# A fused attention and softplus MLP kernel: fp32 state products, fewer turns, weights loaded ahead, a new order of steps

## The chip, the cores and the metric

The kernel runs on one core of a Trainium2 chip. Its time is the device time of one execution in microseconds (us), and several executions are timed. The engines are PE (TensorE, matrix products; PEld is its weight load), DVE (VectorE), ACT (ScalarE), POOL (GpSimd) and SP (SyncE, which here only issues DMAs). Each engine works through its own instructions in program order and waits on semaphores for the others.

## The reference: what is computed

Eight batches of eight heads attend between 512 tokens and 32 state rows, both ways; the result, 8 x 544 rows of 512, goes through an MLP with softplus. The two weight matrices arrive as 64-bit floats, tokens and state as 32-bit ones; the result has 32 bits.

```python
scores = scale * x @ state^T            # per batch and head, 512 x 32
xread  = softmax(scores, over state rows) @ state
scores2 = scale * state @ x^T           # 32 x 512
sread  = softmax(scores2, over tokens) @ x
rows   = concatenate([xread, sread])    # 544 rows a batch, 512 columns over the heads
h   = rows @ w_in                       # 512 -> 2048
g   = maximum(h, 0) + log1p(exp(-abs(h)))
out = g @ w_out                         # 2048 -> 512
```

## The kernel before

**Token rows.** For the 512 token rows of a batch the kernel does not form `xread`. It first makes V = state . w_in for each head ("state products"), and then h = V^T a^T, where a is the softmax over the state rows. So the MLP's first product (`gemm1`, L454) has V as its stationary and the transposed attention `aT` as its moving operand. The hidden features are cut into 16 slots of 128 for each batch. A slot is: six products into a PSUM bank `h`, the softplus (three activations on ACT, L438 to L440, and one addition on DVE, L441, which I call the slot's softplus addition), the split of its result into `ghi` and `glo`, and twelve products with `w_out` into four `acc` banks (`gemm2`, L461). Up to three slots wait between the two products.

**Split operands.** PE multiplies a tile of type float32r faster than one of float32, but with fewer bits. So an operand is split into two parts of 12 bits (`split`: a copy to float32r on ACT or POOL, L92 or L85, and the remainder on DVE or POOL, L93), and a product takes three passes, high by high, high by low and low by high (`PASSES`). `MOVED` is a table of names: a step whose name is in it goes to the other engine than the one that the code names first.

**64-bit weights.** `as_f32` turns a block of 64-bit words into float32. One engine scales the high word (L112 on POOL or L114 on ACT), and three DVE operations (L124 to L126) take the sign bit, shift the low word in, and put the fields together; or, for the blocks that `MOVED` names, two DVE operations (L118, L121), a Sign activation (L120) and a product on POOL (L122).

**State products.** w_in is taken in four chunks of 512 hidden features, each of four blocks q of 128 rows. For chunk 0 and batches 0 to 3, `make_v0` multiplies fp32 operands (`QZ`, the padded state, L167 and L176); batches 0 and 1 are copied to SBUF (`vf`), 2 and 3 go to DRAM (`Vd0`). For chunks 1 to 3, and for all chunks of batches 4 to 7, `make_v` splits each head's weights into parts that stand one above the other (`head`, L218 and L219, tiles `zhl` or `R`), multiplies twice by the split state (`product`, L204), copies the bank to `ve` and writes it to DRAM (L210). `fetch_v` brings a batch's chunk back to `vf` in four pieces, and `split_v` splits it (`vhl`). The converted weights are also written to DRAM (`wsc`), for later batches and for the state's own rows.

**Turns.** `w_in` and `w_out` come in during the first two batches, so those take turns by quarters of the hidden features: eight turns of four slots. After each turn the four `acc` banks are copied to, or added to, sums in SBUF (L549, L552).

**Order.** The order of the work is written out by hand, a letter a step: `START` for batches 0 to 2 and the first 32 slots, `BLOCK` for each later batch, `LAST` for the end; `ATT` gives the order of the steps within a batch's attention. A scheduler then sets each engine's own order from it. All DMAs go through SP's queue, in order, each waiting there until its data or its buffer is ready.

## Time and profile before

| | |
|---|---|
| median of 3 runs | 726.08 us (726.03 to 726.4) |
| span of the profiled execution, first to last instruction | 723.7 us |
| PE, PEld busy | 669.6 us (93%), 538.4 us (74%) |
| DVE, ACT, POOL busy | 526.1 us (73%), 484.9 us (67%), 217.2 us (30%) |
| moved by DMA | 89.76 MB, 124 GB/s over the span |
| mean granted TensorE clock | 0.991 |

The page gives no other time of the profiled execution than its span; the runs' time is that of whole executions. "Busy" is the time in which at least one instruction of the engine runs. Products on PE overlap, so one shows some 390 ns where the next starts 227 ns later, and a busy PE need not be at its peak. In rows of groups, the columns are line, engine, operation, out<-in by the program's names, shape and count, then busy time in us and the mean of one in ns, then idle time of the engine ahead of them and who ended it. Names are without the buffer's number: `wout5` and `wout12` read `wout`, `k2` and `k4` read `k`.

### The profile page before, as it was taken

The numbers are of one execution on the slowest core, as the hardware profiler recorded it, in microseconds if no ns is written. First come the engines' busy times: TensorE is split into PE (matmuls) and PEld (weight loads), VectorE is DVE, ScalarE is ACT, GpSimd is POOL, SyncE is SP. The second block draws the span as 40 slices with busy tenths as digits, with TensorE's granted clock in tenths as the row PEclk, the third lists the DMA queues.
The fourth block names the chain that finished last, engine by engine and source line by source line (L and its number), as shares of the span: only waits on it lengthen the run. The fifth ranks groups of instructions, "written<-read, shape, count | busy, mean of one in ns | idle before, by whom it ended". The sixth has DMA issues, their size and how long they took to land.

```text
span 723.7 us, 9466 instructions
## 1 busy us (share of the span) xinstructions
PE 669.6 (93%) x3012; PEld 538.4 (74%) x3012; DVE 526.1 (73%) x881; ACT 484.9 (67%) x897; POOL 217.2 (30%) x218
## 2 busy tenths in 40 slices
PE   3777869799799999999999999999999999999997
PEld 1445657577687787887888888888888889988886
DVE  4889888999999999569874975498558744534322
ACT  3565868576767787778786776667666676656653
POOL 2456466645754421022110411141113101012100
PEclk9999999999999999999999999999999999999999
DMA  8777727565632645436442421141112112522001
GB/s 293 232 230 246 242 92 257 171 211 163 191 95 95 209 140 178 124 102 203 153 131 88 145 59 59 30 146 30 29 30 87 30 30 73 161 87 60 1 0 59
DMA packets 46194, 89.76 MB, mean 124 GB/s; under 512 B 6976, under 2 KB 13888, under 8 KB 46144
## 3 DMA queue, kind: packets, MB, share of 16 engines
q1 hardware_dynamic: 46144, 89.15, 38.7%
q8 instruction: 24, 0.39, 0.2%
q14 instruction: 26, 0.21, 0.1%
HBM read 60.29 MB, written 28.84 MB: 123 GB/s over the span
## 4 chain that ended last, share of the span: by engine, by line
PE 56%; DVE 26%; ACT 5%; issue 5%; DMA 2%; POOL 2%; SPq 0%; DVEq 0%; ACTq 0%; POOLq 0%
PE acc L461 33%; PE h L454 15%; PE h L501 3%; DVE t L441 3%; DVE glo L93 2%; DVE k L93 2%; PE aux L204 2%; DVE zhl L219 2%; DVE wt L126 2%; DVE k L125 2%; DVE vhl L93 2%; DVE k L124 1%; DVE k L328 1%; PE aux L387 1%; ACT t L438 1%
## 5 line engine op out<-in xcount | busy, mean ns | idle before, releaser
L461 PE MATMUL acc<-wout,ghi 128*128 128x512 f32 x1088 | 339.7, 393 | 3.5 <-DVE o L144 1.0
L461 PEld LDWEIGHTS acc<-wout,ghi 128*128 128x128 f32 x1088 | 203.0, 189 | 48.1 <-DVE o L144 2.0
L461 PE MATMUL acc<-wout,glo 128*128 128x512 f32 x544 | 212.4, 391 | 0.8 <-DVE glo L93 0.8
L454 PE MATMUL h<-aT,vhl 128*128 128x512 f32 x768 | 198.4, 397 | 12.2 <-DVE t L441 9.7
L454 PEld LDWEIGHTS h<-aT,vhl 128*128 128x128 f32 x768 | 144.1, 190 | 46.1 <-DVE t L441 9.8
L441 DVE SCALAR_TENSOR_TENSOR t<-h,t 128x512 f32<-128x512 f32 x136 | 93.2, 686 | 91.9 <-ACT t L440 91.2
L438 ACT ACTIVATE t<-h 128x512 f32<-128x512 f32 x136 | 80.8, 595 | 90.6 <-PE h L454 80.0
L461 PEld LDWEIGHTS acc<-wout,glo 128*128 128x128 f32 x544 | 102.5, 188 | 23.1 <-DVE glo L93 1.4
L93 DVE TENSOR_TENSOR glo<-t,ghi 128x512 fp32r<-128x512 f32 x98 | 75.0, 765 | 36.1 <-ACT ghi L92 21.0
L85 POOL TENSOR_SCALAR ghi<-t 128x512 fp32r<-128x512 f32 x51 | 34.5, 676 | 221.8 <-DVE t L441 189.9
L440 ACT ACTIVATE t<-t 128x512 f32<-128x512 f32 x136 | 85.6, 631 | 2.4
L439 ACT ACTIVATE t<-t 128x512 f32<-128x512 f32 x136 | 85.7, 632 | 1.4
L92 ACT CAST ghi<-t 128x512 fp32r<-128x512 f32 x85 | 52.7, 620 | 48.3 <-DVE t L441 37.4
L93 POOL TENSOR_TENSOR glo<-t,ghi 128x512 fp32r<-128x512 f32 x38 | 51.5, 1357 | 103.1 <-ACT ghi L92 93.1
L93 DVE TENSOR_TENSOR vhl<-vf,vhl 128x512 fp32r<-128x512 f32 x70 | 55.3, 792 | 29.7 <-ACT vhl L92 29.2
L92 ACT CAST vhl<-vf 128x512 fp32r<-128x512 f32 x69 | 42.2, 613 | 13.9 <-PE h L501 8.6
L209 ACT COPY ve<-aux 128x512 f32<-128x512 f32 x41 | 23.2, 579 | 3.5 <-PE aux L204 1.9
L204 PE MATMUL aux<-zhl,wout 128*128 128x512 f32 x48 | 16.1, 420 | 10.0 <-DVE ve L207 4.1
L501 PEld LDWEIGHTS h<-sreadT,vhl 128*128 128x128 f32 x192 | 24.1, 191 | 0.6
L501 PE MATMUL h<-sreadT,vhl 128*128 128x256 f32 x192 | 24.3, 283 | 0.0
L219 DVE TENSOR_TENSOR R<-wt,R 64x512 fp32r<-64x512 f32 x32 | 22.5, 704 | 2.4 <-ACT R L218 1.4
L126 DVE SCALAR_TENSOR_TENSOR wt<-k,k 128x512 int32<-128x512 int32 (+1 forms) x30 | 21.9, 730 | 2.2 <-POOL wout L93 1.2
(139 smaller groups left out, 745.9 us busy)
## 6 DMA issues: line engine op xcount, KB each, us to landing
vd<-ve SPq DMA_DIRECT2D x56, 256.0 KB, 2.3
vf<-vd SPq DMA_DIRECT2D x112, 128.0 KB, 2.8
xT<-in_xt_dram SPq DMA_DIRECT2D x16, 512.0 KB, 4.5
x<-in_xn_dram SPq DMA_DIRECT2D x16, 512.0 KB, 3.9
k<-in_w_out_dram SPq DMA_DIRECT2D x16, 512.0 KB, 3.8
k<-in_w_in_dram SPq DMA_DIRECT2D x12, 512.0 KB, 4.3
out_dram<-o SPq DMA_DIRECT2D x24, 256.0 KB, 2.1
wt<-wsc SPq DMA_DIRECT2D x16, 256.0 KB, 3.1
```

Source lines behind the costliest of these rows:

```text
L85: nc.gpsimd.tensor_scalar(dst, src, 1.0, 0.0, ALU.mult, ALU.add)
L92: nc.scalar.copy(hi, src)
L93: vec(*what).tensor_tensor(lo, src, f32(hi), ALU.subtract)
L126: nc.vector.scalar_tensor_tensor(r.bitcast(I32), h2.bitcast(I32), 3, u, ALU.logical_shift_left, ALU.bitwise_or)
L219: vec("R", *what, o).tensor_tensor(r[z], wf[a], f32(r[a]), ALU.subtract)
L438: nc.scalar.activation(t, h, AF.Abs)
L439: nc.scalar.activation(t, t, AF.Exp, scale=-1.0)
L440: nc.scalar.activation(t, t, AF.Ln, bias=1.0)
L441: nc.vector.scalar_tensor_tensor(t, h, 0.0, t, ALU.max, ALU.add)
L454: nc.tensor.matmul(h, Vhl[b, ft // 2][:, vi, g, cs], aT[b][:, ai, g], start=(n == 0), stop=(n == 5))
L461: nc.tensor.matmul(acc[c], g[gi][:, c0:c0 + P], wout[ft][:, wi], start=(ft == first and i == 0), stop=(ft == last and i == 2))
L501: nc.tensor.matmul(h[:, 256 * i:256 * i + 256], Whl[u, i][:, wi, kt, :], sreadT[:, si, kt, :], start=(n == 0), stop=(n == 11))
```

## The change

The change does five things.

1. *fp32 state products* for chunks 1 to 3 of batches 0 to 3 (`make_vf` in place of `make_v(0, ...)`): two fp32 products a block, as in chunk 0, in place of eight of split operands on four heads' halves. The half for batches 0 and 1 is copied to tiles in SBUF, under the names of `wout` buffers that aren't in use yet, and is no longer written to DRAM and fetched; the half for batches 2 and 3 is written in one piece and fetched in two.
2. *Half the turns*: batches 0 and 1 take five turns of 4, 8, 8, 8 and 4 slots in place of eight of 4.
3. *Weights loaded ahead*: new letters `i` and `o` issue the load of the next block of w_in or w_out; conversion takes the oldest one loaded. The first eight half blocks of w_in have eight buffers. Token inputs `x` are loaded by new steps `L` of the attention and no longer at the very start.
4. *Conversion*: one activation (Prelu with a slope of -2^32 for negative values, so that the sign arrives in the exponent's top bit) and two DVE operations, always.
5. *A new order*: `LOADS`, `ATT`, `START`, `BLOCK` (with `BLOCK2` and `BLOCK3` for batches 2 and 3), `LAST` and `MOVED` are all new.

```diff
-START = 'aaagvavavaBavaaavaaaaaaapabvWaWva|vVVVVVbWbV|pbVb|bVbbVbgbgW|VVVgpbb|V|VVbpgVVWbV|bWgbF|gWVWVpbbg|gVp|gVVVV||FgbVpVVV||VVWgVgWVpVVV|WVVg|gVFVWVVggp|V|VVVVVVpggF|gCVp|cg||WgpFcWgpWWcpF||gg|c||cF|cgcccgcpgcpc|g|cccccc|gg|cpcccgc'
+START = 'aavvaaavaaavaavgavaaBoaWaboapbaaobaWvaa|ibvgVbiVoWVbVVVpbiVbbV|bbaVipWo|iVbbggVVV|VoWiiWpbgVV|VbioVb|Vgbpigo|g|Vbb|WpgbgW|oVVi|VVVVVViiVg|bVpg|pWVo|WVVVgVoVVVo|VWgVpV|WiVgo|Vgg|gpop|g|CgV|VoVgcW|ppcg|og|cW|VcVgoWVW|pVcgcpgg|ccc|cgFgccc|gcccc|pcccp|ccgc|cgc'
...
-    def as_f32(t, *what):
+    def as_f32(t, tag="wt"):
...
         h2 = sb("k2", [P, n], bufs=K2)
-        if ("h2",) + what in MOVED:
-            nc.gpsimd.tensor_scalar(h2, f32(hi), 2.0 ** -112, 0.0, ALU.mult, ALU.add)
-        else:
-            nc.scalar.activation(h2, f32(hi), AF.Copy, scale=2.0 ** -112)
...
-        nc.vector.tensor_scalar(u, hi, SIGN, None, ALU.bitwise_and)
-        nc.vector.scalar_tensor_tensor(u, lo, 29, u, ALU.logical_shift_right, ALU.bitwise_or)
-        nc.vector.scalar_tensor_tensor(r.bitcast(I32), h2.bitcast(I32), 3, u,
-                                       ALU.logical_shift_left, ALU.bitwise_or)
+        nc.scalar.activation(h2, f32(hi), AF.Prelu, scale=2.0 ** -112, alpha=-(2.0 ** 32))
+        r = sb(tag, [P, n], bufs=2 if tag == "wt" else 1)
+        u = r.bitcast(I32)
+        nc.vector.tensor_scalar(u, lo, 29, None, ALU.logical_shift_right)
+        nc.vector.scalar_tensor_tensor(u, h2.bitcast(I32), 3, u, ALU.logical_shift_left, ALU.bitwise_or)
         return r
...
-    QZ = [sb("QZ", [P, 4, P]), sb("zhl", [P, 4, P], bufs=2)]
+    VTAGS = {1: ("wout10", "wout11"), 2: ("wout13", "wout14"), 3: ("vf", "vf")}
+    QZ = [sb("QZ", [P, 4, P]), sb("wout15", [P, 4, P])]
...
+    def load_ahead(k):
+        if coming[k]:
+            come[k].append(load_w(coming[k].pop(0)))
+
+    def ahead(k):
+        if not come[k]:
+            load_ahead(k)
+        return come[k].pop(0)
+
+    def make_vf(cs):
+        for c in cs:
+            for b in range(2):
+                Vf[b, c] = sb(VTAGS[c][b], [P, 2, 512], bufs=2 if c == 3 else 1)
+            for q in range(4):
+                wf = as_f32(ahead("in"), tag="wout12" if (4 * c + q) % 3 == 2 else "wt")
+                nc.sync.dma_start(wsc[c][P * q:P * q + P, :], wf)
+                yield
+                pb = aux()
+                nc.tensor.matmul(pb, QZ[0][:, q, :], wf, start=True, stop=True)
+                r = slice(64 * (q % 2), 64 * (q % 2) + 64)
+                for b in range(2):
+                    dst, src = Vf[b, c][r, q // 2], pb[64 * b:64 * b + 64]
+                    if ("vd", c, q, b) in MOVED:
+                        nc.vector.tensor_copy(dst, src)
+                    else:
+                        nc.scalar.copy(dst, src)
+                made["v", c] = q
+                yield
+                pb = aux()
+                nc.tensor.matmul(pb, QZ[1][:, q, :], wf, start=True, stop=True)
+                ve = sb("ve", [P, 512], bufs=2)
+                if ("ve", 0, c, 2 * q + 1) in MOVED:
+                    nc.vector.tensor_copy(ve, pb)
+                else:
+                    nc.scalar.copy(ve, pb)
+                nc.sync.dma_start(Vd[0, c][:, q, :], ve)
+                made[0, c] = q
+                yield
...
-        w = as_f32(load_w(w_out[P * ft:P * ft + P, :]), ft)
+        w = as_f32(ahead("out"))
...
+            if what == "L":
+                load_x(b, g)
...
-    slots = [(b, ft) for f0 in range(0, NFT, QTR) for b in (0, 1) for ft in range(f0, f0 + QTR)]
+    turns = [(0, 0, 1), (1, 0, 2), (0, 1, 3), (1, 2, 4), (0, 3, 4)]
+    slots = [(b, ft) for b, q0, q1 in turns for ft in range(QTR * q0, QTR * q1)]
```

How the new order moves instructions shows best on three queues. First DVE, behind the first slot's softplus addition, where chunk 1 of w_in is converted. Before (`k` are blocks and scratch, `wt` the converted block, `zhl` the split halves):

```order
L124 TENSOR_SCALAR k_120_425<-k_118_421 128x512
L125 SCALAR_TENSOR_TENSOR k_120_425<-k_118_421,k_120_425 128x512
L93 TENSOR_TENSOR glo_391<-t_385,ghi_390 128x512
L126 SCALAR_TENSOR_TENSOR wt_426<-k_119_423,k_120_425 128x512
L118 TENSOR_SCALAR k_126_441<-k_124_437 128x512
L93 TENSOR_TENSOR vhl_631<-vf_130,vhl_631 128x512
L219 TENSOR_TENSOR zhl_432<-wt_426,zhl_432 64x512
L121 SCALAR_TENSOR_TENSOR k_126_441<-k_125_439,k_126_441 128x512
L441 SCALAR_TENSOR_TENSOR t_480<-h_473,t_480 128x512
```

And now, at the same place, between the first and the third slot's addition (L465):

```order
L114 TENSOR_SCALAR wt_396<-k_98_373 128x512
L170 COPY ve_389<-aux_387 128x256
L115 SCALAR_TENSOR_TENSOR wt_396<-k_107_394,wt_396 128x512
L91 TENSOR_TENSOR vhl_445<-vf_120,vhl_445 128x512
L114 TENSOR_SCALAR wout_120_432<-k_110_404 128x512
L465 SCALAR_TENSOR_TENSOR t_476<-h_469,t_476 128x512
L114 TENSOR_SCALAR wt_415<-k_83_314 128x512
L115 SCALAR_TENSOR_TENSOR wout_120_432<-k_119_430,wout_120_432 128x512
L115 SCALAR_TENSOR_TENSOR wt_415<-k_114_413,wt_415 128x512
```

The third operation of a conversion and the remainders of the split halves (L219) are gone; in their place stand further conversions, of the next block of w_in and of w_out.

Second PE, at the products of that chunk. Before, with `zhl` the split weights of one head, `wout` the two parts of the split state (in buffers that `w_out` takes later) and `aux` the bank:

```order
L204 MATMUL aux_497<-zhl_431,wout_114_411 128x512
L204 MATMUL aux_497<-zhl_431,wout_115_412 128x512
L317 MATMUL aux_503<-xT_200,Z_73 128x512 x2
L204 MATMUL aux_526<-zhl_432,wout_114_411 128x512
L204 MATMUL aux_526<-zhl_432,wout_115_412 128x512
L461 MATMUL acc_556<-wout_87_324,glo_391 128x512
L454 MATMUL h_585<-aT_118,vhl_489 128x512 x6
```

Now, with `QZ` and `wout_2` the padded state of batches 0 and 1, and 2 and 3, and `wt` or `wout_120` a converted block:

```order
L478 MATMUL h_514<-aT_113,vhl_445 128x512 x2
L200 MATMUL aux_406<-wt_396,QZ_87 128x512
L211 MATMUL aux_420<-wt_396,wout_2_88 128x512
L478 MATMUL h_514<-aT_113,vhl_445 128x512 x3
L200 MATMUL aux_436<-wout_120_432,QZ_87 128x512
L211 MATMUL aux_440<-wout_120_432,wout_2_88 128x512
L478 MATMUL h_514<-aT_113,vhl_445 128x512
```

Two fp32 products serve a whole block, and they stand between the passes of a slot's first product.

Third SP, from the start. Before:

```order
L274 DMA xT_90<-in_xt_dram 128x1024
L98 DMA k_4_92<-in_w_in_dram 128x256
L98 DMA k_5_94<-in_w_in_dram 128x256
L98 DMA k_6_96<-in_w_in_dram 128x256
L286 DMA Z_73<-in_zp_dram 128x2x64 x2
L279 DMA x_100<-in_xn_dram 128x1024
L616 DMA zhl_89<-in_zq_dram 128x512
L616 DMA QZ_88<-in_zq_dram 128x512
```

Now:

```order
L295 DMA xT_89<-in_xt_dram 128x1024
L307 DMA Z_73<-in_zp_dram 128x2x64 x2
L97 DMA k_4_93<-in_w_in_dram 128x256
L97 DMA k_5_95<-in_w_in_dram 128x256
L295 DMA xT_97<-in_xt_dram 128x1024
L97 DMA k_7_99<-in_w_in_dram 128x256
L97 DMA k_8_101<-in_w_in_dram 128x256
L97 DMA R_103<-in_w_in_dram 128x256
L644 DMA QZ_87<-in_zq_dram 128x512
```

The padded state for the scores (`Z`) and the second half of the transposed tokens (`xT`) now stand ahead of most weights, and the token rows (`x`) behind all of these.

More of the change, by code (lines that the diff above doesn't have):

```diff
@@ L163, in make_v0 @@
             for q in range(4):
-                wt = as_f32(first.pop(0), 0, half, q)
+                k = 4 * half + q
+                wt = as_f32(first.pop(0), tag=f"wout{4 + k}" if k < 6 else "wt")
                 nc.sync.dma_start(wsc[0][P * q:P * q + P, cs], wt)
@@ L181, in make_v0 @@
                     nc.scalar.copy(ve, pb[:, 0:256])
-                nc.sync.dma_start(Vd0[:, q, cs], ve)
+                nc.sync.dma_start(Vd[0, 0][:, q, cs], ve)
                 made["v0", half] = q
                 yield
-    StK = {}
-    def prep_stk(g4, tags):
-        if len(tags) > 1:
-            k = [sb(tag, [P, H, P], F32R) for tag in tags]
-        else:
-            t = sb(tags[0], [P, 2, H, P], F32R)
-            k = [t[:, 0], t[:, 1]]
-        StK[g4] = k
+    coming = {"in": [w_in[c, q] for c in range(1, 4) for q in range(4)],
+              "out": [w_out[P * ft:P * ft + P, :] for ft in range(NFT)]}
@@ new lines, in attention_then_softplus_mlp @@
+    come = {"in": [], "out": []}
+    def load_ahead(k):
[34 more added lines that the diff above has]
+                yield
@@ L430, in split_wout @@
     def split_wout(ft):
-        assert ft < NFT - 2 or all(made[0, c] == H for c in range(1, 4))
+        assert ft < NFT - 1 or all(made[0, c] == 3 for c in range(1, 4))
         wout[ft] = sb(f"wout{ft}", [P, 2, DM], F32R)
-        w = as_f32(load_w(w_out[P * ft:P * ft + P, :]), ft)
+        w = as_f32(ahead("out"))
         split(wout[ft][:, 0], wout[ft][:, 1], w, "wout", ft)
@@ L531, in flush @@
             return
-        first = ft // QTR * QTR if b < 2 else 0
-        last = first + QTR - 1 if b < 2 else NFT - 1
+        first, last = next(r for r in runs.get(b, [(0, NFT - 1)]) if r[0] <= ft <= r[1])
         if ft == first:
@@ L554, in flush @@
                     nc.sync.dma_start(d, p)
-    fetches = [(fetch_w, (ft,)) if b == B else (fetch_v, (b, ft // 4)) for b, ft in slots if b == B or ft % 4 == 0][2:]
+    fetches = [(fetch_w, (ft,)) if b == B else (fetch_v, (b, ft // 4)) for b, ft in slots if b == B or ft % 4 == 0 and b > 1]
     pieces = [(split_w, (ft,)) if b == B else (split_v, (b, ft // 2)) for b, ft in slots if b == B or ft % 2 == 0]
-    wt_tags = [f"wout{NFT - 2 + i}" for i in range(2)]
     first = []
@@ L597, in run @@
                     break
+            elif what in "io":
+                load_ahead({"i": "in", "o": "out"}[what])
             elif what == "g":
@@ L606, in attention_then_softplus_mlp @@
     v0 = make_v0()
-    v_first = chain(lambda: prep_stk(0, wt_tags), lambda: make_v(0, V_ORDER, RTAGS, VLAG[0]))
-    v_second = chain(lambda: prep_stk(1, ["StK"]), lambda: make_v(1, range(4), ["R"], VLAG[1]))
+    v_first = make_vf(range(1, 4))
+    v_second = chain(prep_stk, lambda: make_v(range(4), 2))
     att[0] = attention(0, ATT[0])
```

104 lines of the change are left out of this document (43 added, 61 removed).

## The prediction

> **What bounds the kernel now.** I read the page's 40 slices first, to see whether one engine limits the whole span.
>
> ```profile
> span 723.7 us, 9466 instructions
> ...
> PE   3777869799799999999999999999999999999997
> DVE  4889888999999999569874975498558744534322
> POOL 2456466645754421022110411141113101012100
> ```
>
> It does not: there are two regimes. In the first dozen slices DVE shows 9, PE 6 to 9 and POOL 4 to 7; from about slice 14 on PE shows 9 and DVE falls away. So the next view is busy time by stretch. I cut at the softplus additions (L441, one for each slot of 128 hidden features), because they mark progress on DVE: the first starts at 45.1 us, the thirteenth at 122.7, the thirty-third, batch 2's first, at 234.1.
>
> ```profile
> L441 DVE SCALAR_TENSOR_TENSOR t<-h,t x12: 676/682/692, 45.1 to 115.7; 128x512 f32<-128x512 f32 x12
> L441 DVE SCALAR_TENSOR_TENSOR t<-h,t x32: 668/681/692, 45.1 to 225.3; 128x512 f32<-128x512 f32 x32
> ```
>
> ```profile
> core 0: us, PE busy (x) PEld busy (x) DVE busy (x) ACT busy (x) POOL busy (x), PEclk, DMA share, GB/s
> 0.00:45.10 45.10, 26.30 (x84) 16.69 (x84) 29.76 (x71) 21.21 (x50) 18.98 (x27) 0.92 0.80 258
> 45.10:122.70 77.60, 62.54 (x250) 45.62 (x251) 70.75 (x97) 54.94 (x106) 45.38 (x39) 0.98 0.62 207
> 122.70:234.10 111.40, 99.12 (x426) 77.68 (x426) 106.18 (x163) 74.22 (x138) 62.30 (x54) 0.98 0.49 157
> 234.10:314.30 80.20, 78.22 (x351) 63.04 (x350) 64.36 (x115) 63.45 (x117) 16.78 (x17) 1.00 0.52 166
> 314.30:723.70 409.40, 403.47 (x1906) 335.39 (x1904) 255.07 (x439) 271.07 (x490) 73.75 (x82) 1.00 0.25 76
> ```
>
> The columns of the second fence are stretch, its length, then busy time and instructions of PE, weight load, DVE, ACT and POOL, then the granted clock and the DMA share. In the second and third stretch DVE is busy for 70.8 of 77.6 and 106.2 of 111.4 us; from 314.3 on it is PE, 403.5 of 409.4, and DVE has a third of its time free. The granted clock, 0.92 to 1.00, explains little of it. The chain that ends last, in the window from 45 to 234 us, says the same by line:
>
> ```profile
> by line: issue 10.2%; DVE zhl L219 7.1%; DVE k L125 6.1%; DVE wt L126 6.1%; DVE glo L93 5.8%; DVE t L441 5.8%; PE h L454 5.6%; DVE k L124 4.5%; PE acc L461 3.8%; DVE wout L93 3.3%; DVE k L93 3.2%; DVE vhl L93 3.0%; DMA k<-in_w_in_dram 1.9%;
> ```
>
> L124 to L126 are the conversion of 64-bit weights, L219 the remainders of the weights split for the state products, and both are DVE's. So the place where this change can earn is the first 234 us; in the 490 us after that, work taken from DVE or ACT is hidden under PE, and work added to PE shows in full.
>
> **The change on DVE.** Mean durations of the operations concerned:
>
> ```profile
> L124 DVE TENSOR_SCALAR k<-k 128x512 int32<-128x512 int32 x24 | 14.8, 617 | 0.1
> L125 DVE SCALAR_TENSOR_TENSOR k<-k,k 128x512 int32<-128x512 int32 x24 | 19.8, 826 | 0.3
> L126 DVE SCALAR_TENSOR_TENSOR wt<-k,k 128x512 int32<-128x512 int32 x24 | 19.5, 811 | 2.2 <-POOL wout L93 1.2 <-issue 0.5 <-DVE k L125 0.2
> L126 DVE SCALAR_TENSOR_TENSOR wt<-k,k 128x256 int32<-128x256 int32 x6 | 2.4, 406 | 0.0
> L219 DVE TENSOR_TENSOR zhl<-wt,zhl 64x512 fp32r<-64x512 f32 x16 | 17.3, 1083 | 2.3 <-ACT zhl L218 1.3 <-POOL zhl L85 0.5
> L93 DVE TENSOR_TENSOR wout<-wt,wout 128x512 fp32r<-128x512 f32 x9 | 9.9, 1100 | 1.8 <-ACT wout L92 1.8
> L93 DVE TENSOR_TENSOR glo<-t,ghi 128x512 fp32r<-128x512 f32 x98 | 75.0, 765 | 36.1 <-ACT ghi L92 21.0 <-POOL ghi L85 13.8
> L207 DVE COPY ve<-aux 128x512 f32<-128x512 f32 x15 | 10.1, 678 | 0.2 <-PE aux L204 0.2
> L552 DVE TENSOR_TENSOR StK<-acc,StK 128x512 f32<-128x512 f32 x12 | 7.8, 673 | 0.0
> ```
>
> The conversion of 28 blocks of 512 columns takes three DVE operations in 24 cases and two in 4; the new one always takes two, a shift (as L124) and a shift with or (as L125). That is 24 operations less, at 0.82 us 19.7 us; 6 of 256 columns go as well, at 0.41, 2.5 us. The products of batches 0 to 3 no longer split weights: 16 remainders on DVE at 1.08, 17.3 us. Half the turns leave 12 additions of parked sums instead of 24: 12 at 0.67, 8.1 us. Together 47.6 us, nearly all ahead of 234 us, where DVE has 206.7.
>
> They do not all fall in the same stretch, so I counted the two orders up to the thirteenth softplus addition. Both have 168 DVE rows there (71 and 48 of them ahead of the first), since loading ahead pulls conversions forward. Conversions: shifts 17 to 23 (+6 at 0.62, +3.7), shift-with-or 31 to 23 (-8 at 0.82, -6.6), 256-wide ones -2.4. Split remainders 9 to 0 (-9.7). Remainders of w_out 4 to 9 (+5.5), of the softplus result 7 to 10 (+2.3), evacuations of PSUM 2 to 6 (+2.7), small ones +2. Net -2.5: 100.5 us of busy time becomes 98. Between the thirteenth and the thirty-third the rest falls: 21 shift-with-ors and 11 shifts become 5 and 5 (24.0 to 7.2), 7 remainders at 1.08 and 12 additions go; 106.2 becomes 106.2 - 16.8 - 7.6 - 8.1 = 73.7.
>
> Means hide a second effect, the time that DVE is held up by POOL:
>
> ```profile
> L125 DVE SCALAR_TENSOR_TENSOR k<-k,k x30: 406/685/1668, 7.1 to 190.3; 128x512 int32<-128x512 int32 x24, 128x256 int32<-128x256 int32 x6
> L219 DVE TENSOR_TENSOR zhl<-wt,zhl x16: 685/985/1673, 49.8 to 162.9; 64x512 fp32r<-64x512 f32 x16
> L93 POOL TENSOR_TENSOR glo<-t,ghi x38: 1267/1296/1796, 67.5 to 691.8; 128x512 fp32r<-128x512 f32 x38
> ```
>
> The columns are minimum, median and maximum in ns. An undisturbed shift-with-or takes 685, but some take 1668. The difference, 983, is less than one POOL subtraction, 1267 at least. POOL was busy for 64.4 us of the first 122.7; in the new order only 15 large rows stand there, 9 subtractions or products, 12 us at the median of 1.3, and 6 copies, which take no longer each: 12 to 20 us. So operations that stay get shorter. How much is not in the trace: nothing at the least; at the most the excess of mean over median on what stays in that stretch: 23 shift-with-ors at 0.14, 9 w_out remainders at 0.4 (1100 against the undisturbed 685), some 75 others at 0.07, together 12. I take 7, a little over the middle, as POOL keeps about a quarter of its work.
>
> The Trainium skill, "SBUF — State Buffer", section "Who interferes with whom", says that a DVE instruction with two SBUF inputs and a GpSimd instruction that reads SBUF take one port pair in turn, and that whichever comes second waits until the first is done. By that rule, as an estimate, all 12 us would go with POOL's rows, and the forecast would be 5 us lower. That a held operation exceeds its median by less than one POOL subtraction agrees with it.
>
> **The change on ACT.** The means:
>
> ```profile
> L114 ACT ACTIVATE k<-k 128x512 f32<-128x512 f32 x19 | 12.6, 667 | 2.8 <-DMA k<-in_w_out_dram 2.8
> L218 ACT CAST zhl<-wt 64x512 fp32r<-64x512 f32 x15 | 9.2, 615 | 0.6 <-PE aux L204 0.5
> L209 ACT COPY ve<-aux 128x512 f32<-128x512 f32 x41 | 23.2, 579 | 3.5 <-PE aux L204 1.9 <-DMA vd<-ve 1.0 <-ACT sr L395 0.5
> L327 ACT COPY k<-aux 64x512 f32<-64x512 f32 x24 | 13.9, 578 | 2.2 <-DVE k L328 1.6 <-PE aux L323 0.3
> ```
>
> Ahead of the thirteenth softplus ACT's rows go from 144 to 166: first steps of conversions 11 to 28 (they came partly from POOL), 13 at 0.67 and 4 of half width, +10.4; copies of 64 rows out of the new products, 18 at 0.58 as for the 64-row copy L327, +10.4; split copies -10 at 0.61, -6.2; evacuations -3.4; parked sums -2.4; others +4.5. Net +13: 76.2 becomes 89.5. The activation that carries the sign is priced as the scaling copy that it replaces, 0.67, bounded by ACT's other 512-column work at 0.58 and 0.67. Over the rest of the start ACT loses about 10 of 74.2. The batches after it gain some 8 us of copies from POOL, under PE.
>
> **The change on PE.** It gets dearer.
>
> ```profile
> 11.57 0.59 PE L176 MATMUL acc<-wt,zhl 128*128 128x256 f32 x2
> 12.00 0.59 PE L167 MATMUL acc<-wt,QZ 128*128 128x256 f32 x2
> 560.51 0.61 PE L461 MATMUL acc<-wout,ghi 128*128 128x512 f32 x2
> 561.19 0.61 PE L461 MATMUL acc<-wout,ghi 128*128 128x512 f32 x2
> L204 PE MATMUL aux<-zhl,wout 128*128 128x512 f32 x48 | 16.1, 420 | 10.0 <-DVE ve L207 4.1
> ```
>
> An fp32 product of 256 columns starts 0.43 us after the last one (11.57, 12.00), so 512 columns take 0.86. Three products of split operands take 0.68 (560.51 to 561.19), 0.227 each. Of 48 split products 24 fp32 ones are left: +20.6 - 10.9 = +9.7 us, 20 of the 24 in the first stretch. There PE's own time, from the order's counts, is 180 split products (40.8), 20 new fp32 ones (17.2), 16 of 256 columns for the first chunk and as many in the read (13.8), 8 scores (6.9) and transposes (2): 81 us. In the next stretch it has 20 slots of 18 products (81.7), 4 fp32 products (3.4) and batch 2's attention (about 6): 91.
>
> **DMA and SP.** Twelve writes of products go, and 48 small fetches become 12 larger ones, for two batches no longer pass through DRAM:
>
> ```profile
> vd<-ve SPq DMA_DIRECT2D x56, 256.0 KB, 2.3
> vf<-vd SPq DMA_DIRECT2D x112, 128.0 KB, 2.8
> ```
>
> That takes 5 us of latency off the first use of a chunk, which DVE's backlog covers today. Loads of x move behind the first conversions, and w_in and w_out are issued some blocks ahead of use. In the first stretch the volume stays about the same: six more blocks of 512 KB against the writes and fetches saved. At 258 and 207 GB/s it fits into a somewhat shorter stretch. I cost all this at nothing; if it does not hold, it is the second rival.
>
> **The sum.** First stretch: DVE 98 - 7 = 91 busy, plus the 22.2 that it idles today (15.3 of them before the first softplus, where it waits for loads and the attention's chain): 113. ACT: 89.5 plus its 24 idle ahead of the first softplus, 113 to 114. PE's 81 is covered. I take 114 against 122.7, with 108 (all blocking gone, first softplus 4 us sooner) and 122 (two engines equally full wait for each other) as ends. Second and third together: PE is now the longest with 91, against DVE 74 and ACT 64. In the stretch from 234.1, where DVE and ACT stand at 64 of 80, PE is busy for 78.2 of 80.2; with attention work crowding the end I take 8 us of loss: 99 against 111.4, ends 94 and 107. The rest I leave at 489.6; its products are the same. So 723.7 - 8.7 - 12.4 = 702.6 for the span. The median of the runs, 726.08, is 2.4 above the span of the profiled execution, and what lies around the span stays: 705.0.
>
> **Rivals.** First, more than that: DVE's start shrinks because the first softplus no longer waits behind 31 us of DVE work, POOL's hold is gone, and PE runs at its own time. With both lower ends, 108 and 94, the span is 691.6 and the time 694. For it speaks how long a held operation takes, 1668 against 685; against it that ACT gets fuller exactly there.
>
> Second, the relief is eaten: with DVE, ACT and PE at 91, 90 and 81 of 114, waits pass from one to the other, or loads come late. The waits of the start show the links:
>
> ```profile
> PE h L454 <- DVE t L441: 9.7, 4, 3.9
> PE aux L204 <- DVE ve L207: 4.1, 4, 1.6
> SPq L210 <- ACT ve L209: 65.4, 27, 6.3
> ```
>
> With 122 and 107 the span is 718.6, the time 721; half that is 713. Against it: PE waited only 4.1 us for copies of the 24 products.
>
> Third, slower, by one mechanism: a converted block now holds its buffer until both fp32 products and the write to DRAM have read it, where a split released it. DVE converts in order, so a block whose buffer is taken stops softplus additions behind it; the products wait for a bank, the bank for ACT's three copies. There are 12 such blocks, and the forecast lies 21 us below today, so from 1.8 us a block on the kernel is slower; if each waits for a whole product and three copies, 0.86 + 3 x 0.58 = 2.6 us, it takes 705 + 31 = 736. Against it: the blocks take turns in three buffers, and SP's queue already waits 65 us for such copies, 27 times, behind which nothing stood still for long.
>
> Fourth, no change: if the start is a chain of latencies and not DVE's fill, the kernel saves perhaps the 10 us of the lighter rows ahead of the first softplus, and PE's 9.7 us eat them: 725 to 727. DVE at 94% from 45 to 234 us (176.9 of 188.9) speaks against it.
>
> **How the numbers follow.** A change within 0.2%, 1.5 us, could not be told from none. The forecast, 698 to 713: 0.55. More than that, below 698: 0.16. Eaten, 713 to 724.6: 0.20. Same: 0.03. Slower: 0.06. So faster 0.91. The range leaves out the worst of the second rival with all of the third and the tail of the first: 693 to 719.
>
> **What would show it.** In the new profile the thirteenth softplus should start near 114 us and the thirty-third near 213; DVE busy near 88 to 100 us in the first of these and near 74 in the next, POOL under 25 in the first; shift-with-or means near 0.70; PE at 9 from about slice 7 on; fp32 products 0.86 apart; stretch after 234 no longer than now. If the thirteenth comes after 120 with DVE idle for over 30, the relief went into waits; if PE idles for over 15 in the next stretch, loads or evacuations took the lead. A second table load on ACT would make all of it wrong.

## Result and profile after

The changed kernel takes 707.63 us (median of 4 runs, 706.78 to 713.27) against 726.06 for the one before (725.87 to 726.4). The ratio of the runs is put at 0.9765, with a 95% interval from 0.973 to 0.9799 (the two medians alone give 0.975). The profiled execution took 708.3 us with a span of 706.3. The prediction said 705.0, with 693 to 719 as its range.

The first lines of the page of the changed kernel, as shown of the one before:

```profile
span 706.3 us, 9196 instructions
...
PE   5679999999999999999999999999999999999997
DVE  4499768936798997796858754875487534544322
...
POOL 1221102665233565201201070107010510000220
```

PE shows 9 from the fourth slice on; before, it did so without a break only from the twelfth on. DVE's unbroken block of 8s and 9s (slices 2 to 16) is broken up, and in the first dozen slices POOL has about half the work that it had.

The softplus additions (now L465) as marks of progress, in two windows that end just ahead of the thirteenth and the thirty-third:

```profile
L465 DVE SCALAR_TENSOR_TENSOR t<-h,t x12: 646/684/692, 39.4 to 112.3; 128x512 f32<-128x512 f32 x12
L465 DVE SCALAR_TENSOR_TENSOR t<-h,t x32: 646/687/692, 39.4 to 205.0; 128x512 f32<-128x512 f32 x32
```

The first starts at 39.4 us (before 45.1). The next after these rows, the thirteenth and the thirty-third, start at 117.8 (122.7) and 211.0 (234.1). Busy time in the stretches between these marks, columns as in the prediction:

```profile
0.00:39.40 39.40, 23.60 (x70) 13.94 (x70) 18.65 (x49) 17.63 (x41) 8.65 (x14) 0.96 0.79 270
39.40:117.80 78.40, 75.43 (x274) 50.21 (x275) 65.00 (x121) 70.91 (x138) 12.04 (x12) 0.98 0.78 253
117.80:211.00 93.20, 93.02 (x414) 75.33 (x413) 68.67 (x114) 64.80 (x118) 42.37 (x40) 1.00 0.28 86
211.00:706.30 495.30, 488.64 (x2258) 396.48 (x2256) 313.96 (x538) 347.98 (x620) 109.77 (x106) 1.00 0.28 90
```

Take PE's idle time, length minus first busy column. Before it was 18.8, 15.1, 12.3 and 7.9 us in the four stretches, 54.1 in all; now it is 15.8, 3.0, 0.2 and 6.7, together 25.6. PE's busy time rose from 669.6 to 680.7. So the change took 28.5 us of waiting from PE and made its busy time 11.1 us longer (4.1 ahead of the thirty-third addition, 7.0 behind it), which makes the 17.4 us by which the span fell. The 23.1 us won at the thirty-third addition are not all kept: the rest of the run takes 495.3 us where it took 489.6. The chain of work that ended last, between 39 and 211 us, by line:

```profile
by line: PE acc L485 38.6%; PE h L478 20.8%; PE aux L200 3.3%; ACT wout L207 3.2%; ACT ghi L90 2.3%; PE aux L211 2.1%; ACT k L111 2.0%; issue 1.9%; ACT t L463 1.9%; ACT t L462 1.8%; ACT t L464 1.7%; PE aux L411 1.2%; PE aux L405 1.1%; DVE k
```

Conversion and remainders on DVE led before; gemm2 (L485) and gemm1 (L478) lead now.

### The profile page after: what moved, and what is told of

Its sections match the earlier page's. It is cut to its first block, busy times and chain, and to the rows that moved or that the text cites. A ratio compares the mean times of both kernels' runs of the same rounds, so it can differ in the third digit from the quotient of the medians.

```text
span 706.3 us, 9196 instructions
## 1 busy us (share of the span) xinstructions
PE 680.7 (96%) x3012; PEld 536.0 (76%) x3012; DVE 466.3 (66%) x818; ACT 501.3 (71%) x914; POOL 172.8 (24%) x170
## 4 chain that ended last, share of the span: by engine, by line
PE 81%; ACT 9%; DVE 7%; issue 2%; DMA 1%; POOL 0%; SPq 0%; ACTq 0%; DVEq 0%; POOLq 0%
PE acc L485 47%; PE h L478 22%; PE h L525 3%; PE aux L235 2%; PE aux L411 1%; ACT t L463 1%; ACT t L462 1%; ACT t L464 1%; ACT ghi L90 1%; PE aux L341 1%; PE aux L347 1%; DVE k L91 1%; PE aux L392 1%; DMA xT<-in_xt_dram 1%; PE aux L200 1%
## 5 line engine op out<-in xcount | busy, mean ns | idle before, releaser
L485 PE MATMUL acc<-wout,ghi 128*128 128x512 f32 x1088 | 343.1, 394 | 0.9 <-DVE StK L577 0.5
L485 PEld LDWEIGHTS acc<-wout,ghi 128*128 128x128 f32 x1088 | 203.2, 188 | 48.2 <-issue 2.4
L485 PE MATMUL acc<-wout,glo 128*128 128x512 f32 x544 | 214.1, 394 | 0.0
L478 PE MATMUL h<-aT,vhl 128*128 128x512 f32 x768 | 203.7, 402 | 4.3 <-DVE t L465 3.8
L478 PEld LDWEIGHTS h<-aT,vhl 128*128 128x128 f32 x768 | 142.2, 189 | 44.4 <-DVE t L465 9.6
L465 DVE SCALAR_TENSOR_TENSOR t<-h,t 128x512 f32<-128x512 f32 x136 | 93.1, 686 | 97.4 <-ACT t L464 97.1
L485 PEld LDWEIGHTS acc<-wout,glo 128*128 128x128 f32 x544 | 102.1, 188 | 22.7 <-issue 0.7
L91 DVE TENSOR_TENSOR glo<-t,ghi 128x512 fp32r<-128x512 f32 x100 | 70.3, 703 | 35.4 <-ACT ghi L90 14.8
L90 ACT CAST ghi<-t 128x512 fp32r<-128x512 f32 x104 | 64.5, 620 | 36.4 <-PE acc L485 23.2
L91 DVE TENSOR_TENSOR vhl<-vf,vhl 128x512 fp32r<-128x512 f32 x62 | 47.1, 760 | 36.0 <-ACT vhl L90 34.0
L83 POOL TENSOR_SCALAR ghi<-t 128x512 fp32r<-128x512 f32 x32 | 21.7, 679 | 180.7 <-PE acc L485 139.8
L91 POOL TENSOR_TENSOR glo<-t,ghi 128x512 fp32r<-128x512 f32 x36 | 48.5, 1351 | 49.6 <-ACT ghi L90 43.1
L90 ACT CAST vhl<-vf 128x512 fp32r<-128x512 f32 x59 | 36.4, 616 | 18.1 <-PE h L525 11.7
L368 POOL TENSOR_TENSOR T<-T,sm 128x512 f32<-128x512 f32 x13 | 15.1, 1160 | 120.7 <-DVE sm L367 92.3
L111 ACT ACTIVATE k<-k 128x512 f32<-128x512 f32 (+1 forms) x32 | 20.2, 645 | 10.3 <-DMA k<-in_w_in_dram 7.7
L352 DVE TENSOR_TENSOR k<-aux,k 64x512 f32<-64x512 f32 x24 | 16.4, 682 | 12.5 <-ACT k L351 12.3
L115 DVE SCALAR_TENSOR_TENSOR wt<-k,wt 128x512 int32<-128x512 int32 (+1 forms) x26 | 20.2, 791 | 2.0 <-ACT k L111 1.7
```

The source lines that it names most:

```text
L83: nc.gpsimd.tensor_scalar(dst, src, 1.0, 0.0, ALU.mult, ALU.add)
L90: nc.scalar.copy(hi, src)
L91: vec(*what).tensor_tensor(lo, src, f32(hi), ALU.subtract)
L111: nc.scalar.activation(h2, f32(hi), AF.Prelu, scale=2.0 ** -112, alpha=-(2.0 ** 32))
L115: nc.vector.scalar_tensor_tensor(u, h2.bitcast(I32), 3, u, ALU.logical_shift_left, ALU.bitwise_or)
L465: nc.vector.scalar_tensor_tensor(t, h, 0.0, t, ALU.max, ALU.add)
```

## Experiments

The theory to test was the prediction's: DVE's fill set the start, and DVE relieved, PE's own time sets it. The kernels below undo or add one part each. A scheduler orders the instructions anew after each edit, so I take differences of 3 us or so between two kernels as possibly its doing. All times are medians; differences are against the 707.63 of the changed kernel unless said otherwise.

**The new conversion alone, in the kernel before.**

```diff
...
-            nc.scalar.activation(h2, f32(hi), AF.Copy, scale=2.0 ** -112)
...
-        nc.vector.tensor_scalar(u, hi, SIGN, None, ALU.bitwise_and)
-        nc.vector.scalar_tensor_tensor(u, lo, 29, u, ALU.logical_shift_right, ALU.bitwise_or)
-        nc.vector.scalar_tensor_tensor(r.bitcast(I32), h2.bitcast(I32), 3, u,
-                                       ALU.logical_shift_left, ALU.bitwise_or)
+        nc.scalar.activation(h2, f32(hi), AF.Prelu, scale=2.0 ** -112, alpha=-(2.0 ** 32))
+        u = r.bitcast(I32)
+        nc.vector.tensor_scalar(u, lo, 29, None, ALU.logical_shift_right)
+        nc.vector.scalar_tensor_tensor(u, h2.bitcast(I32), 3, u, ALU.logical_shift_left, ALU.bitwise_or)
```

> The kernel before with one part of the change alone: the new conversion, one activation and always two DVE operations. Theory (DVE's own time sets the start): DVE loses 24 operations of 0.82 us and 6 of 0.41, 22 us, and POOL 15 copies and 6 products; the thirty-third softplus addition comes 12 to 20 us sooner than 234.1 and the kernel takes 708 to 715. Rival (a chain of loads, products and softplus sets the start, DVE is only full beside it): 722 to 726. Second rival (ACT, which now takes the scalings from POOL, becomes the bound): 726 to 732.

Measured: 720.97 us (720.52 to 722.62), ratio 0.9923 [0.9902, 0.9944], a gain of 5 us where 11 to 18 were expected, and close to the rival's 722. DVE's busy time fell by 29 us in all, from 526.1 to 497.1. In its windows between the first, thirteenth and thirty-third additions:

```profile
48.50:121.70 73.20, 62.65 (x250) 46.07 (x250) 54.64 (x84) 56.52 (x109) 34.64 (x31) 0.95 0.63 218
121.70:231.20 109.50, 100.89 (x425) 78.83 (x426) 97.09 (x153) 74.84 (x138) 58.30 (x51) 0.97 0.48 160
```

DVE is busy for 54.6 of 73.2 us and 97.1 of 109.5, where it had 70.8 of 77.6 and 106.2 of 111.4, and yet the second stretch is only 1.9 us shorter. The shift's group in this kernel says where part of the time went:

```profile
L114 DVE TENSOR_SCALAR wt<-k 128x512 int32<-128x512 int32 x28 | 14.5, 519 | 10.7 <-POOL wout L93 7.4 <-DMA wsc<-wt 2.0 <-POOL zhl L207 1.2
```

The shift now writes the converted block's own buffer, so it waits 10.7 us until earlier readers of it are done, POOL's remainders above all. A DVE that was busy for 94% of a stretch was not its only limit: in the old order most of what it saved became waiting (DVE idles for 223.7 us of this span, 197.6 before). How much of that is this claim on the buffer, and how much the old order, isn't separated.

**The old conversion, in the changed kernel.**

```diff
-        nc.scalar.activation(h2, f32(hi), AF.Prelu, scale=2.0 ** -112, alpha=-(2.0 ** 32))
+        nc.scalar.activation(h2, f32(hi), AF.Copy, scale=2.0 ** -112)
...
-        nc.vector.tensor_scalar(u, lo, 29, None, ALU.logical_shift_right)
+        nc.vector.tensor_scalar(u, hi, -2147483648, None, ALU.bitwise_and)
+        nc.vector.scalar_tensor_tensor(u, lo, 29, u, ALU.logical_shift_right, ALU.bitwise_or)
```

> The changed kernel with the old conversion: a scaling copy on ACT and always three DVE operations, 28 of 512 and 8 of 256 columns more on DVE, 23 us, nearly all ahead of 140 us. Theory (PE and ACT set the changed kernel's start, DVE has 13 of 78 us free in the first stretch): 8 to 14 us slower than the changed kernel, 715 to 721. Rival (DVE no longer matters once PE leads at 39 us): 707 to 710. If DVE is still what counts: 728 to 731.

Measured: 718.85 us (718.13 to 720.26), 0.9892 [0.9871, 0.9913], 11.2 us more.

```profile
41.60:127.30 85.70, 76.76 (x276) 50.22 (x275) 77.69 (x144) 70.44 (x136) 12.93 (x12) 0.98 0.72 234
```

DVE has 17.5 us more in all, and 77.7 of the 85.7 us between the first and the thirteenth addition. So the new conversion is worth 11 us in the new order and 5 in the old one, where it also moved scalings from POOL to ACT.

**Every fp32 product done twice.**

```diff
-                nc.tensor.matmul(pb, QZ[0][:, q, :], wf, start=True, stop=True)
+                for _ in range(2):
+                    nc.tensor.matmul(pb, QZ[0][:, q, :], wf, start=True, stop=True)
...
```

> The changed kernel with each of the 24 fp32 products done twice (same result): PE has 20.6 us more, 17 of them in the first stretch; every other engine has the same work. Theory (from the first softplus on PE is the chain): 15 to 20 us slower than the changed kernel, 722 to 728. Rival (ACT and DVE set the first stretch and PE's 81 us have cover there): 707 to 713.

Measured: 731.98 us (731.05 to 732.46), 1.0069 [1.005, 1.0088], 24.4 us more for 20.6 us of products.

```profile
41.00:140.20 99.20, 94.25 (x320) 59.14 (x321) 70.06 (x127) 75.14 (x141) 12.18 (x13) 0.98 0.66 218
```

The stretch to the thirteenth addition grew from 78.4 to 99.2 us, with PE busy for 94.3 of it. PE has no room there to hide work. Four rows of PE show the price, two products each (two records a product):

```profile
50.09 1.95 PE L201 MATMUL aux<-wt,QZ 128*128 128x512 f32 x4
51.88 1.88 PE L213 MATMUL aux<-wt,wout 128*128 128x512 f32 x4
53.64 1.96 PE L201 MATMUL aux<-wout,QZ 128*128 128x512 f32 x4
55.43 1.96 PE L213 MATMUL aux<-wout,wout 128*128 128x512 f32 x4
```

From 50.09 to 55.43 stand six products, 0.89 us each; the prediction had 0.86.

**One fp32 product a block instead of two.**

```diff
-                pb = aux()
-                nc.tensor.matmul(pb, QZ[1][:, q, :], wf, start=True, stop=True)
```

> The changed kernel with one fp32 product a block in place of two (that for batches 2 and 3 is left out, and their state products are copied from the first one's bank): PE has 10.3 us less, ACT, DVE and the DMAs have the same work. Theory (PE is the chain): 8 to 10 us faster than the changed kernel, 698 to 700. Rival (ACT, with 71 of 78 us in the first stretch, is next to PE): 3 to 5 us faster, 703 to 705.

Measured: 702.49 us (701.47 to 704.22), 0.9671 [0.9648, 0.9695], 5.1 us less for 10.3 us of products.

```profile
38.70:114.10 75.40, 68.24 (x261) 47.90 (x262) 63.54 (x120) 69.48 (x136) 13.19 (x12) 0.98 0.81 270
```

PE now idles for 7.2 us of the stretch, and ACT, with 69.5 of 75.4, is the fullest. So PE leads by some 5 us, and ACT stands next.

**The load of split products, with and without that product.** Both kernels add this to each block, the first on top of the kernel with one product:

```diff
...
+    both = sb("wout15", [P, 2, 512])
...
+    def resplit(wf, o):
+        a, z = slice(64 * o, 64 * o + 64), slice(64 - 64 * o, 128 - 64 * o)
+        r = both[:, 1].bitcast(F32R)
+        nc.scalar.copy(r[a], wf[a])
+        nc.vector.tensor_tensor(r[z], wf[a], f32(r[a]), ALU.subtract)
...
+                for o in range(2 if (4 * c + q) % 3 == 0 else 1):
+                    resplit(wf, o)
```

> The changed kernel with the loads of the old state products: the second fp32 product of each of the 12 blocks left out (batches 2 and 3 get copies of the first bank, as in the earlier kernel with one product), PE -10.3 us, and 16 halves of the converted blocks split into a scratch tile, 16 casts on ACT at 0.61 and 16 remainders on DVE at 0.69 to 1.08, ACT +9.8, DVE +11 to +17. Theory (in the new order the fp32 products pay, since what they free on ACT and DVE counts for more than their 10 us on PE): ACT would need 82 of the first stretch's 78.4 us, so the time is 709 to 716, above the changed kernel's 707.6. Rival (PE's own time decides and the other engines have room): 700 to 706, so that the fp32 products alone cost time.

> The changed kernel with the same 16 casts on ACT and 16 remainders on DVE added and both fp32 products kept: what the split work costs by itself in the new order. Theory (ACT at 70.9 and DVE at 65.0 of 78.4 us are close behind PE there): 8 to 13 us more, 715 to 721, nearly all of it ahead of the thirteenth softplus addition. Rival (hidden beside PE): 707 to 710.

Measured: 715.82 us (713.9 to 718.82), 0.9858 [0.9834, 0.9882], for the first, 8.2 more than the changed kernel; 718.71 (717.63 to 719.09), 0.9892 [0.9878, 0.9906], for the second, 11.1 more. Their stretch between the first and the thirteenth addition, of the first and then of the second:

```profile
41.20:121.70 80.50, 69.91 (x259) 48.57 (x260) 71.87 (x129) 74.51 (x145) 12.83 (x12) 0.96 0.72 235
```

```profile
38.20:125.00 86.80, 79.67 (x274) 53.31 (x275) 73.23 (x132) 76.99 (x149) 13.34 (x12) 0.92 0.70 229
```

In the first, PE idles for 10.6 us, with ACT at 74.5 and DVE at 71.9 of 80.5: the stretch is longer than any engine's busy time in it, and I read this as two engines nearly full that wait for each other. The effects nearly add up: 11.1 for the split work less 5.1 for the product makes 6.0, and 8.2 was measured. The fp32 products cost PE 10 us and still pay.

**POOL made busy again in the first stretch.**

```diff
...
+    both = sb("wout15", [P, 2, 512])
...
+    def hold(c, q):
+        r = slice(64 * (q % 2), 64 * (q % 2) + 64)
+        v = Vf[0, c][r, q // 2]
+        nc.gpsimd.tensor_tensor(both[r, 1], v, v, ALU.mult)
```

It is called three times a block; `both` has the padded state of batches 2 and 3 in its first half, and nothing reads what is written to the second.

> The changed kernel with 36 more POOL products of 64 x 512 (both inputs in SBUF, output unused), three behind each block of the chunks 1 to 3, 47 us of POOL time in the first stretch, where POOL has 66 of 78 us free. Theory (POOL's operations hold DVE's): DVE's shift-with-or and subtractions of the first stretch get longer, means 0.82 to 0.95 against 0.69 undisturbed, DVE's busy time there grows by 8 to 15 us, and the kernel takes 3 to 10 us more than the changed one. Rival (no hold; the long DVE operations have another cause): means as in the changed kernel and 706 to 709.

Measured: 723.77 us (721.7 to 730.56, 10 runs), 0.9965 [0.9938, 0.9992], 16.1 more. The conversion's two groups and the remainders of w_out in the changed kernel, then with POOL busy:

```profile
L115 DVE SCALAR_TENSOR_TENSOR wt<-k,wt 128x512 int32<-128x512 int32 x24 | 19.5, 821 | 2.0 <-ACT k L111 1.7
L91 DVE TENSOR_TENSOR wout<-wt,wout 128x512 fp32r<-128x512 f32 x14 | 12.2, 868 | 3.7 <-POOL wout L83 2.4 <-ACT wout L90 1.2
L114 DVE TENSOR_SCALAR wt<-k 128x512 int32<-128x512 int32 x24 | 11.5, 488 | 2.3 <-PE aux L211 2.2
```

```profile
L115 DVE SCALAR_TENSOR_TENSOR wt<-k,wt 128x512 int32<-128x512 int32 x24 | 22.7, 955 | 0.9 <-ACT k L111 0.7
L114 DVE TENSOR_SCALAR wt<-k 128x512 int32<-128x512 int32 x24 | 19.4, 817 | 0.7 <-PE aux L219 0.7
L91 DVE TENSOR_TENSOR wout<-wt,wout 128x512 fp32r<-128x512 f32 x14 | 15.3, 1089 | 4.3 <-POOL wout L83 3.2 <-ACT wout L90 1.0
```

With the same number of DVE instructions, 818, and 42.6 us more of POOL work, DVE's busy time rose by 17.6 us, 0.41 for each. The trace shows it operation by operation: of the 28 plain shifts (L114) of 512 columns, the 15 that started while POOL was at work took 634 to 1510 ns, the 13 others 404 to 428. DVE's stretch to the thirteenth addition:

```profile
38.80:130.20 91.40, 80.73 (x277) 52.62 (x278) 80.04 (x121) 71.25 (x138) 47.83 (x42) 0.94 0.65 218
```

DVE takes 80.0 us for the 121 instructions that took 65.0. The Trainium skill, "SBUF — State Buffer", "Who interferes with whom", has the two engines share one port pair; that DVE's operations grow when only POOL gets work agrees with it. PE's 5.3 us more of busy time at a granted clock of 0.94 against 0.98 are a part of the 16 us that this doesn't explain.

**Without loading ahead**: the letters `i` and `o` are taken from `START`, so that a block's load is issued where it is converted.

> The changed kernel without the steps that load w_in and w_out ahead: each block of 512 KB is asked for where it is converted; all else, the tables of the order too, stays. Theory (in the first stretch the engines are 83 to 96% full, so each late block stalls DVE and ACT in order): with some 4.8 us to landing and 23 blocks up to the thirteenth softplus, 8 to 25 us slower than the changed kernel, 715 to 732, with waits of DVE and ACT for the weights' DMA. Rival (four buffers and the queue hide the loads, as before the change): 706 to 710.

Measured: 712.39 us (712.16 to 714.66), 0.9812 [0.9789, 0.9836], 4.8 more, less than expected. The first and thirteenth addition come at 37.8 and 117.8 us, no later than in the changed kernel. What is lost is lost where batch 2's attention is made, from the 25th slot's addition to the 29th's:

```profile
165.90:195.50 29.60, 26.22 (x116) 21.60 (x115) 24.09 (x36) 15.77 (x28) 15.24 (x14) 0.94 0.34 108
```

The waits in the same window have this row:

```profile
PE aux L392 <- ACT e L380: 3.4, 1, 3.4
```

PE idles for 3.4 us there, waiting once for an exponential (line, releaser, us in total, times, longest). In the changed kernel the same piece takes 24.3 us and PE is busy for all of it. How the missing letters lead there isn't shown.

**Eight turns again.**

```diff
-    turns = [(0, 0, 1), (1, 0, 2), (0, 1, 3), (1, 2, 4), (0, 3, 4)]
+    turns = [(b, q, q + 1) for q in range(4) for b in (0, 1)]
```

> The changed kernel with the eight turns of four slots of before: 12 more additions of parked sums on DVE (8.1 us) and three more handovers of the four banks. Theory (PE is the chain from 39 us on, DVE has 24 of 93 us free in the second stretch): the additions are hidden, 1 to 4 us slower, 708 to 712. Rival (each handover stalls PE for its copies, since all four banks turn at once): 3 times 2.7 us, 714 to 717.

Measured: 711.0 us (709.48 to 711.85), 0.979 [0.9767, 0.9813], 3.4 more: as expected, though no more than a new order alone can do.

**Products ahead of the first scores.** In the changed kernel PE's first products take twice as long as the same ones later (columns: start, duration, engine, line, count):

```profile
4.95 3.75 PE L341 MATMUL aux<-xT,Z 128*128 128x512 f32 x4 [4.95 <-DMA Z<-in_zp_dram]
9.76 3.54 PE L341 MATMUL aux<-xT,Z 128*128 128x512 f32 x4 [1.05 <-DMA xT<-in_xt_dram]
...
26.50 3.68 PE L405 MATMUL acc<-x,a2T 128*128 128x256 f32 x8 [1.60 <-ACT a2T L395]
...
31.34 1.99 PE L405 MATMUL h<-x,a2T 128*128 128x256 f32 x8 [0.73 <-ACT a2T L395]
33.17 1.88 PE L341 MATMUL aux<-xT,Z 128*128 128x512 f32 x4
```

Two kernels give PE work that nobody reads, so that it doesn't idle. The first one:

```diff
...
-                nc.tensor.matmul(pb[:, 0:256], QZ[1][:, q, :], wt, start=True, stop=True)
+                for _ in range(2 if k < 6 else 1):
+                    nc.tensor.matmul(pb[:, 0:256], QZ[1][:, q, :], wt, start=True, stop=True)
...
+                if b == 0 and g == 0:
+                    pb = aux()
+                    for _ in range(5):
+                        nc.tensor.matmul(pb[:, 0:256], Z4[:, 0, :], xTin[b, g][:, 0, 0:256], start=True, stop=True)
...
+    for _ in range(4):
+        nc.tensor.matmul(pb[:, 0:256], busy[:, 0:P], busy[:, 0:256], start=True, stop=True)
...
```

> The changed kernel with products that nobody reads in PE's gaps of the first 25 us: four on a zeroed tile before the first loads land, five between the scores of the two groups, and the second product of the first six half blocks done twice. Theory (the scores at 5 and 10 us took 3.75 and 3.54 for four halves and the first read 3.68, against 1.88 and 1.99 later, because the granted clock is low after idle stretches, and all three stand on the chain to the first softplus): these take 1.9 to 2.1, the first softplus starts 2 to 4 us sooner, the kernel takes 703 to 706. Rival (loads and DVE set the first softplus, or PE's added work delays what it should speed up): 707 to 710.

Measured: 714.79 us (713.71 to 714.98), 0.9835 [0.9815, 0.9855], 7.2 more. The read did take 1.98 us, but the scheduler put a half-block product ahead of the first gemm1, and PE waited there for its conversion:

```profile
26.11 1.98 PE L410 MATMUL acc<-x,a2T 128*128 128x256 f32 x8
...
40.12 1.22 PE L158 MATMUL acc<-wt,QZ 128*128 128x256 f32 x2 [7.59 <-DVE wt L115]
```

The first softplus addition came at 48.5 us. So I chose repeats that leave PE's order at the start as it was (none between the scores, and `2 <= k < 6`):

> The changed kernel with four products on a zeroed tile ahead of the first scores, and the second product of four of the first chunk's half blocks done twice. In this version, as in the changed kernel, PE takes all but the last two half blocks, then the transposes and the read of the first attention, and only then the first slot; the earlier version had half-block products ahead of the transposes. Theory (the first products run at half speed because PE has idled, and the first softplus addition waits for that chain): scores of 1.9 us in place of 3.75 and 3.54, a read of 2.0 in place of 3.68, the first softplus addition 2 to 4 us sooner, at 35 to 37 us, and the time 703 to 706. Rival (the chain ahead of the first slot is set by loads, conversions and the softmax on DVE and ACT, whose orders move as well): the first softplus addition at 38 to 41 us and the time 706 to 711.

Measured: 707.22 us (706.39 to 707.51), 0.9729 [0.9712, 0.9745]. That interval and the changed kernel's overlap, and the medians are 0.4 us apart; it is no better. The first rows of PE and the first read:

```profile
1.45 3.78 PE L638 MATMUL aux<-a2T 128*128 128x256 f32 x8 [1.45 <-DVE a2T L635]
5.04 2.38 PE L342 MATMUL aux<-xT,Z 128*128 128x512 f32 x4
10.06 1.96 PE L342 MATMUL aux<-xT,Z 128*128 128x512 f32 x4 [2.64 <-DMA xT<-in_xt_dram]
...
25.36 1.99 PE L406 MATMUL acc<-x,a2T 128*128 128x256 f32 x8 [1.34 <-ACT a2T L396]
```

DVE just ahead of the first softplus addition (L466 here):

```profile
37.97 1.03 DVE L114 TENSOR_SCALAR wt<-k 128x512 int32<-128x512 int32 x1
38.92 0.28 DVE L114 TENSOR_SCALAR wt<-o 128x256 int32<-128x256 int32 x1
39.24 0.69 DVE L466 SCALAR_TENSOR_TENSOR t<-h,t 128x512 f32<-128x512 f32 x1
```

The second score and the read run at full speed, the first score nearly so, and the first gemm1 starts at 33.57 us instead of 35.25. But the first softplus addition starts at 39.24, as good as no earlier: two shifts of the conversion had come ahead of it on DVE. So the rival's forecast holds: both scores and the read together take 4.6 us less, of which 1.7 are left at the first gemm1 and next to nothing at the first softplus addition.

**Four copies from ACT to DVE**: `("vd", 1, 0, 1)`, `("vd", 1, 2, 1)`, `("vd", 2, 0, 1)` and `("vd", 2, 2, 1)` are added to `MOVED`.

> The changed kernel with four of the 64-row copies out of the fp32 products (chunks 1 and 2, blocks 0 and 2, batch 1) on DVE in place of ACT: ACT -2.3 us, DVE +2.7 in the first stretch, where they are busy for 70.9 and 65.0 of 78.4. Theory (ACT stands next to PE there, as the kernel with one product a block in place of two showed, which gained 5.1 of 10.3 us): the thirteenth softplus addition 1 to 2 us sooner and the time 705 to 707.5. Rival (PE alone sets that stretch, or DVE's queue holds the copies behind conversions): no gain or a loss of up to 3 us, 707.5 to 711.

Measured: 710.98 us (709.71 to 711.39), 0.9782 [0.9764, 0.98], 3.4 more. The thirteenth addition comes at 118.2. The chain in the window from 39 to 118 us, by line:

```profile
by line: issue 9.4%; PE acc L485 9.0%; DVE wt L115 7.5%; ACT wout L207 6.8%; ACT k L111 5.9%; ACT t L463 5.5%; ACT t L462 4.5%; DVE wt L114 3.9%; PE h L478 3.8%; ACT ghi L90 3.7%; ACT t L464 3.5%; PE aux L405 2.5%; ACT StK L574 2.4%; DVE wo
```

DVE's conversion (L115, L114) stands in it with 11.4%, beside gemm2's 9.0%; in the changed kernel L115 has 2.2% of that window's chain and gemm2 17.5%. That is the rival's forecast, by its second reason. No version tried here that computes the whole result is clearly faster than the changed kernel.

## Why the prediction was right, and where it wasn't

*Where the gain would fall.* Ahead of the thirty-third addition, as said: 23.1 us there, and a loss of 5.7 behind it.

*What sets the start.* The prediction took DVE's own time as the limit. It was one of several. Freed alone, DVE's 29 us gave 5 (first experiment). The gain needs the relief and the new order together; how much the order alone would give wasn't tried.

*First stretch, 114 forecast, 117.8 measured.* The engines came out near the sums: ACT 88.5 busy against 89.5, POOL 20.7 against "under 25", DVE 83.6 against 91. The step that failed is "PE's 81 is covered". From 39.4 us on PE is busy for 75.4 of 78.4, and more products lengthen the run by at least their own time (24.4 for 20.6). PE was busy for 99.0 us of the first 117.8, where 81 were counted. About 5 of the difference are first products that run at half speed, and 5 more that PE had by then done 196 split and 22 fp32 products where 180 and 20 were counted; the rest isn't split up. DVE could end at 114; PE, which also idles for 15.8 us ahead of the first addition, could not.

*Blocking by POOL, 7 us taken of at most 12.* This was too small. At the 0.41 measured, the 43.7 us by which POOL's busy time fell ahead of the thirteenth addition (64.4 to 20.7) are worth 18. From the 98 counted, that gives 80; measured were 83.6. The bound was too low: it gave 0.07 us to each operation outside two groups, but the plain shift took 617 ns on average before, with a median of 419. Nor did the gain come where I looked for it: shift-with-or took 821 ns on average, 826 before, though 0.70 was forecast.

```profile
L115 DVE SCALAR_TENSOR_TENSOR wt<-k,wt x26: 424/691/1780, 36.8 to 139.3; 128x512 int32<-128x512 int32 x24, 128x256 int32<-128x256 int32 x2
```

Half of these took 691 ns or less (the columns are minimum, median and maximum). Of the 28 shift-with-ors of 512 columns six took more than 1 us, and each of these started while a POOL instruction ran; without POOL at work none took more than 695. The Trainium skill's rule, weighed in the prediction, gives the better DVE sum here (86 against the 83.6 measured, where 91 was taken). The time didn't follow, as PE led.

*Second stretch, 99 forecast, 93.2 measured.* DVE 68.7 against 74, ACT 64.8 against 64, and PE 93.0 of 93.2, against an own time of 91. The 8 us set aside for attention work that crowds the end weren't needed. The two misses, +3.8 and -5.8, leave the thirty-third addition at 211.0, forecast 213.

*The rest, 489.6 taken.* This is nearly as large a miss as the second stretch: 495.3. "Its products are the same" was right, but not that they take the same time. The kernel before in that part, to set beside the last of the four rows above:

```profile
234.10:723.70 489.60, 481.68 (x2255) 398.43 (x2253) 319.43 (x553) 334.52 (x606) 90.53 (x99) 1.00 0.29 91
```

At the mark PE still has 2258 products to run, where it had 2255, so the 23.1 us were not won by putting products off past it. But it is busy with them for 488.6 us in place of 481.7: 216.4 ns a product in place of 213.6. It idles for less (6.7 against 7.9), and the granted clock is 1.00 in both. The longer time goes with the new order: the two kernels that keep the old one have 489.6 in that part, the twelve with the new one 493.6 to 496.5. What in the order spaces the products out isn't shown.

*The parts.* Undone one at a time, the conversion is worth 11.2 us, fp32 products against the load of split ones 8.2, loads ahead 4.8 and fewer turns 3.4. That is 27.6, more than the 18.4 of the whole, so they overlap. To put 42.6 us of work back on POOL costs 16.1, more than any of these: by this the relief of POOL, which the prediction had as a term of 7 us, is a large part of the gain, and it overlaps with the conversion, which took scalings off POOL. The conversion's activation costs what the copy did, as said: 675 ns against 667, with one table load in the whole kernel:

```profile
L111 ACT ACTIVATE k<-k 128x512 f32<-128x512 f32 x28 | 18.5, 675 | 2.7 <-DMA k<-in_w_out_dram 2.4 <-DMA k<-in_w_in_dram 0.2
L50 ACT ACT_TABLE_LOAD x1 | 1.3, 1283 | 0.7 <-PEq L696 0.7
```

Loading ahead was costed at nothing; undone, it costs 4.8 us.

*The rivals.* "Eaten" fits the first stretch by its number, 3.8 us more than forecast, but not by its mechanism: PE idles for only 3.0 us from 39.4 to 117.8. "More than that" failed in the first stretch on PE, and held in the second: 93.2, where the lower end was 94. The slower case, blocks that hold their buffers, showed only in small: from 39.4 to 117.8 us a shift of the conversion waits twice on DVE for an fp32 product that still reads its buffer, 2.8 us in all, where the mechanism reckoned with 31. PE waits 0.2 us for the copies of the fp32 products (L207), and 0.9 for a conversion.

```profile
DVE wt L114 <- PE aux L211: 2.2, 1, 2.2
DVE wout L114 <- PE aux L211: 0.6, 1, 0.6
PE aux L200 <- DVE wout L115: 0.9, 1, 0.9
PE aux L211 <- ACT a2T L395: 0.3, 1, 0.3
PE aux L200 <- ACT wout L207: 0.2, 1, 0.2
```
